# Spreading small constants by TensorE products, key sums in four column tiles, stores in pairs on two queues, and a new order of everything

## The chip, the cores and the metric

The kernel runs on one core of a Trainium2 chip. A core has five engines that run side by side: TensorE (PE) for matrix products, VectorE (DVE), ScalarE (ACT), GpSimd (POOL) and SyncE (SP), which here only issues DMAs. ACT issues DMAs too, in line with its own work. The metric is the device time of one execution in microseconds (us), the median of several runs.

## The reference

Two stages follow each other. The first is a linear attention with a product feature map, for 4 batches of 4 heads, 1088 tokens and 32 channels; the second is a two-layer network over the 4352 tokens, with 128 inputs and outputs and 2048 hidden units.

```
a = S1 @ x ; b = S2 @ x                      # 8 numbers each, per token
phi(x) = outer(a, b)                         # 64 features
kv = sum_s phi(k_s) v_s^T ;  z = sum_s phi(k_s)
attn = phi(q) kv / (phi(q) . z + 1e-6)       # per batch and head
x = attn, heads side by side                 # 4352 x 128
h = x @ w_in
out = (max(h,0) + alpha * min(h,0)) @ w_out
```

## The kernel before

All inputs come in as float32. The network is computed in bfloat16 in this form: with g = relu(h), the output is g @ (w_out scaled by 1 − alpha) plus x @ W, where W = w_in @ (w_out scaled by alpha) is computed once (step Wmm). So each 512 tokens need 16 products with w_in (h), 16 relus (r, on ACT or DVE), 16 products with the scaled w_out, w_a (o), one product with W, a transpose out of PSUM (t, on DVE) and a store (s). There are eleven such pieces: 0a, 0b (256 tokens each), 1 to 6 (512 each), 7, 8 and 9 (256 each). Piece 9 multiplies the other way round, so that tokens come out on partitions and no transpose is needed; its two halves of 128 tokens are copied out by t9.0 and t9.1 and stored by s9.0 (SP) and s9.1 (ACT).

Ahead of each piece stands the attention. For the keys of batch b: kbT (a DVE transpose), kbf (the 16 numbers a and b, on TensorE), kbab (transposed back), kbp0 and kbp1 (the products a·b, on DVE or POOL, in tiles kp), kbv (sums of key features with V), kbz, kbzm, kbcw, kbcc (the sums of the keys, folded into the weights fW for the denominators), kbvc, kbvT, kbW (kv laid out as weights). For the queries: qbf, qbg, qbcb, qbs, qbe, qbrc, qbbd (denominators), qbp (products), qbt (transposes), qbn (numerators) and qbx, which is the input of the network. The first 512 tokens of batch 0 go by a shorter path, f0 and f1, so that the network can start early.

Constants are made at the start: ident on POOL, masks from it on DVE, then rowsT on TensorE, which turns S1 and S2 (loaded as rows0 and rows1), and kW, Sab and fW from it. S1rep comes from a third load, rowsS1, and alpha from a load that lays 2048 numbers over the partitions in runs of four. The steps w_in_bf, w_a, w_b, w_hi and w_lo prepare the weights; winT and winTc turn w_in.

The program is a graph of named steps. ORDER is a list, written by a planner, of every step with its engine (`@p` PE, `@d` DVE, `@a` ACT, `@g` POOL, `@s` SP); each engine works its own steps off in the order of that list and waits in place for what a step needs. SLOTS gives each buffer its place; bank 7 of PSUM collects the outputs of one piece after the other, and three buffers oT hold outputs on their way to DRAM. `fill` steps are idle matmuls, and `warm` is a hundred of them. The costs in the graph were used by the planner alone; the kernel on the chip only knows ORDER and SLOTS.

Of the kernel before, what the change touches and what calls it, by code (L numbers as in the profile page):

```python
# [42 lines left out]
class Graph:  # L43


    CLASSES = {"ps": 8, "kT": 2, "kab": 3, "kp": 4, "qT": 2, "gt": 2, "pr": 3, "pt": 2, "dn": 2, "aq": 2, "dt": 2, "rr": 2,
               "rh": 10, "oT": 3, "xT": 4, "zm": 2, "fs": 2, "wb": 2}
    SHAPES = {"kT": ([128, J * 32], F32), "kab": ([128, 9, 2, 32], F32), "kp": ([128, 20, 64], F32),
# [85 lines left out]
    def load(self, name, dst, src, nbytes, eng="sp", rate=290.0, deps=()):  # L134
        def emit(e):
            (self.nc.sync if eng == "sp" else self.nc.scalar).dma_start(dst(), src())
        return self.op("ld." + name, [(eng, 60, 60)], emit, deps, load=nbytes / rate, queue=eng)
# [5 lines left out]
    def loads(self):  # L143
# [3 lines left out]
            f"S{i + 1}", 0, [D, R], [0, H], [1, D]), 4096, "act", 16.0) for i in range(2)]  # L147
# [14 lines left out]
        def v(b, x):  # L162

            n, lo = (9 - x), 18 * x
            return [self.load(f"v{b}.{2 * x + y}", lambda y=y: T[f"v{b}"][64 * x + 32 * y:64 * x + 32 * y + 32, :, x:, :].rearrange("p h j d -> p h (j d)"),
                              lambda y=y: self.dram("v", b * H * S * D + (lo + n * y) * D, [J * D, 32], [S * D, H], [1, n * D]),
                              128 * n * D * 4, rate=260.0) for y in range(2)]
# [8 lines left out]
        for what in self.LOADS:  # L176
# [3 lines left out]
                lambda: self.dram("q", JM * D, [J * D, 128], [H * S * D, B], [1, 2 * D]), 128 * B * 256, rate=150.0)  # L180
# [12 lines left out]
    def constants(self):  # L193
# [8 lines left out]
        def red(dst, src, off, *dims, axis=AX.X):  # L202
# [5 lines left out]
        self.c_mz = self.op("Mz", [("dve", 140, 220)], lambda e: red("Mz", "ident", 0, [2 * R, H], [64, 2], [1, R], axis=AX.XY), [c_id])  # L208
        self.c_e8 = self.op("E8", [("pool", 300, 340), ("dve", 140, 220)], lambda e: self.copy(
            e, self.tl("E8", 0, [64, 2], [8, 8], [1, 8]), self.tl("M8", 0, [0, 2], [1, R], [0, R])), [self.c_m8])  # L210
        b = self.bank()
# [3 lines left out]
            self.tl("kW", 0, [16, 2], [1, 16]), self.ps(b, 0, [0, 2], [1, 16]), self.tl("par2", 0, [1, 2], [0, 16])), [o, self.c_par], [b])  # L215
        self.c_Sab = [self.op(f"Sab{i}", [self.act(64), self.dve(64)], lambda e, i=i: self.copy(
            e, self.tl("Sab", 64 * i, [8, 8], [1, 8]), self.ps(b, 8 * i, *(([1, 8], [0, 8]), ([0, 8], [1, 8]))[i])), [o], [b]) for i in range(2)]
        self.c_S1 = self.op("S1rep", [("pool", 280, 320), ("dve", 210, 290)], lambda e: self.tt(
            e, self.tl("S1rep", 0, [32, 4], [1, 32]), self.tl("rowsS1", 0, [0, 4], [1, 32]), self.tl("Mz", 0, [1, 4], [0, 32]), ALU.mult),
            [L["rowsS1"], self.c_mz], port=1)  # L220
        self.c_fW = self.op("fW", self.ad(128), lambda e: self.copy(e, self.tl("fW", 0, [16, 8], [1, 16]), self.ps(b, 0, [0, 8], [1, 16])), [o], [b])
        self.c_om = self.op("omaT", [("pool", 100, 140), ("dve", 80, 160)], lambda e: (self.nc.vector if e == "dve" else self.nc.gpsimd).tensor_scalar(
            T["omaT"], T["alphaT"], -1.0, 1.0, ALU.mult, ALU.add), [L["alpha"]], port=1)
# [8 lines left out]
    def weights(self):  # L232
# [5 lines left out]
        for i in range(4):  # L238
            def scaled(e, dst, a, i=i):
# [10 lines left out]
                e, self.sb(bw, 0, [DM, 4], [1, DM]), T[f"w_out_f{i}"], self.tl("alphaT", 4 * i, [1, 4], [0, DM]), ALU.mult), [L["alpha"]] + L["w_out", i], [bw], port=1)  # L250
# [21 lines left out]
        o = self.op("Wmm", [self.pe(109 * NC + 10, 170)], wm, lo + wt, [b], ni=32)  # L272
# [6 lines left out]
    def keys(self, b):  # L279
# [18 lines left out]
        else:  # L298
            o = self.op(f"k{b}f", [self.pe(650)], lambda e: feats(e, range(4)), [turns[0], self.c_kW], [bT, bf], ni=32, mode=2)
        o = self.op(f"k{b}ab", [self.dvt(576)], lambda e: nc.vector.transpose(  # L300
            self.sb(bab, 0, [32, 2], [64, 9], [1, 32]), self.ps(bf, 0, [512, 2], [32, 9], [1, 32])), [o], [bf, bab])

        prods = []
        for x, (lo, n) in enumerate(((0, 5), (5, 4))):
            bp = self.buf("kp")

            def pr(e, lo=lo, n=n, bp=bp):
                self.tt(e, self.sb(bp, 0, [64, 4 * n], [8, 8], [1, 8]), self.sb(bab, 64 * lo, [16, 4 * n], [1, 8], [0, 8]),
                        self.sb(bab, 64 * lo + 8, [16, 4 * n], [0, 8], [1, 8]), ALU.mult)
            prods.append((self.op(f"k{b}p{x}", [self.pool(256 * n), self.dve(256 * n)], pr, [o], [bab, bp], port=1), lo, n, bp))  # L310
# [8 lines left out]
        z = self.op(f"k{b}z", [self.pe(310)], zs, [o], [bab, bz], ni=36, mode=1)  # L319
# [5 lines left out]
        o = self.op(f"k{b}cw", [self.pe(230)], lambda e: self.mm(self.ps(bc, 0, [1, 32]), T["S1rep"], self.sb(bzm)), [zm, self.c_S1], [bzm, bc], ni=4, mode=1)  # L325
# [12 lines left out]
        for x, (p, lo, n, bp) in enumerate(prods):  # L338
# [6 lines left out]
            o = self.op(f"k{b}v{x}", [self.pe(128 * n + 30)], kv, [p, o] + L["v", b], [bp, bk], ni=16 * n, mode=1)  # L345
# [399 lines left out]
```

## Time and profile before

| | |
|---|---|
| median of 3 runs | 120.55 us (120.3 to 121.59) |
| profiled execution | 121.51 us, its span 119.7 us |
| PE busy | 102.6 us, 86% |
| DVE, ACT, POOL busy | 82.1, 65.2, 46.3 us |
| read from HBM, written | 8.81 MB, 2.23 MB |
| mean granted clock of TensorE | 0.901 |

The span runs from the first instruction of the profiled execution to the last; the execution's own time holds about 1.8 us more. In the slices of the page one digit stands for a fortieth of the span, 3 us. In the chain and the timeline a row gives the start in us, the duration in us, the engine, the line of the kernel, and output<-input. Tile numbers such as oT__101 tell buffers apart. A window row gives its length, then for each engine busy us and the number of instructions, then the granted clock, the mean busy share of the DMA engines and GB/s. Most matmuls are recorded under one line, that of the helper `mm`, so they are told apart by tiles.

### The profile page before, as it was taken

The numbers are of one execution on the slowest core, as the hardware profiler recorded it, in microseconds if no ns is written. First come the engines' busy times: TensorE is split into PE (matmuls) and PEld (weight loads), VectorE is DVE, ScalarE is ACT, GpSimd is POOL, SyncE is SP. The second block draws the span as 40 slices with busy tenths as digits, with TensorE's granted clock in tenths as the row PEclk, the third lists the DMA queues.
The fourth block names the chain that finished last, engine by engine and source line by source line (L and its number), as shares of the span: only waits on it lengthen the run. The fifth ranks groups of instructions, "written<-read, shape, count | busy, mean of one in ns | idle before, by whom it ended". The sixth has DMA issues, their size and how long they took to land.

```text
span 119.7 us, 3722 instructions
## 1 busy us (share of the span) xinstructions
PE 102.6 (86%) x1559; PEld 61.9 (52%) x1574; DVE 82.1 (69%) x144; ACT 65.2 (54%) x125; POOL 46.3 (39%) x49
## 2 busy tenths in 40 slices
PE   7339889989999998999999999999999999997000
PEld 7214568457776665445445544544444457887000
DVE  3217805789797799878997849779869966674000
ACT  0410136979954686767548447778336637764000
POOL 2011942959999599226940003980010300000000
PEclk9975555599999999999999999999999999999855
DMA  3988999999950002200400000273320000453310
GB/s 109 275 292 239 265 379 274 259 221 234 244 124 11 0 3 38 60 5 9 78 0 5 0 5 0 44 125 55 53 35 5 0 0 0 70 94 52 58 27 16
DMA packets 24096, 11.28 MB, mean 94 GB/s; under 512 B 19088, under 2 KB 21392, under 8 KB 24080
## 3 DMA queue, kind: packets, MB, share of 16 engines
q1 hardware_dynamic: 23136, 10.95, 37.8%
q8 instruction: 12, 0.20, 0.7%
q10 hardware_dynamic: 944, 0.10, 0.6%
q14 instruction: 4, 0.03, 0.1%
HBM read 8.81 MB, written 2.23 MB: 92 GB/s over the span
## 4 chain that ended last, share of the span: by engine, by line
PE 46%; DMA 14%; POOL 11%; DVE 11%; SPq 7%; issue 3%; ACT 2%; ACTq 1%; DVEq 0%; POOLq 0%
PE ps L130 44%; DMA alphaT<-in_moe_alpha_dram 5%; SPq L561 5%; DMA v<-in_v_dram 5%; DVE pr__77 L127 3%; POOL kp__69 L127 2%; POOL w_hl L127 2%; POOL pr__77 L127 2%; POOL kp__70 L127 2%; POOL dn__82 L127 2%; DVE gt__75 L418 2%; DMA out_dram<-oT__101 1%; DMA out_dram<-oT__100 1%; DMA out_dram<-oT__102 1%; SPq L568 1%
## 5 line engine op out<-in xcount | busy, mean ns | idle before, releaser
L130 PEld LDWEIGHTS <-w_in_bf 128*128 128x128 bf16 x176 | 16.8, 98 | 13.1 <-issue 1.3
L130 PE MATMUL ps<-xT__103,w_in_bf 128*128 128x256 bf16 (+1 forms) x94 | 22.2, 325 | 0.5 <-ACT w_in_bf L122 0.2
L130 PEld LDWEIGHTS <-w_a 128*128 128x128 bf16 x160 | 15.4, 98 | 13.3 <-issue 3.0
L130 PE MATMUL ps<-xT__104,w_in_bf 128*128 128x256 bf16 (+1 forms) x62 | 15.6, 325 | 0.1
L516 ACT ACTIVATE rh__91<-ps 128x512 bf16<-128x512 f32 x14 | 8.4, 599 | 3.6 <-PE ps L130 3.5
L516 ACT ACTIVATE rh__93<-ps 128x512 bf16<-128x512 f32 x13 | 7.8, 599 | 4.6 <-PE ps L130 3.9
L516 ACT ACTIVATE rh__92<-ps 128x512 bf16<-128x512 f32 x13 | 7.8, 598 | 3.0 <-PE ps L130 3.0
L127 POOL TENSOR_TENSOR kp__70<-kab__66 128x1024 f32<-128x1024 f32 x3 | 7.2, 2384 | 5.3 <-DVE kab__66 L300 5.2
L516 ACT ACTIVATE rh__90<-ps 128x512 bf16<-128x512 f32 x11 | 6.6, 600 | 4.7 <-PE ps L130 4.7
L127 POOL TENSOR_TENSOR pr__78<-gt__75 128x512 f32<-128x512 f32 x6 | 7.7, 1299 | 0.9 <-DVE gt__75 L127 0.9
L127 POOL TENSOR_TENSOR pr__77<-gt__75 128x512 f32<-128x512 f32 x5 | 5.8, 1170 | 5.1 <-DVE gt__75 L127 4.9
L130 PE MATMUL ps<-const-bfloat16-1.0 128*32 128x32 bf16 (+1 forms) x107 | 6.4, 214 | 1.6 <-issue 0.9
L127 POOL TENSOR_TENSOR dn__82<-gt__75 128x256 f32<-128x256 f32 (+2 forms) x4 | 2.2, 554 | 13.2 <-DVE gt__75 L418 13.2
L518 DVE TENSOR_SCALAR rh__96<-ps 128x512 bf16<-128x512 f32 x9 | 6.1, 676 | 1.3 <-PE ps L130 1.3
L122 ACT CAST w_in_bf<-w_in_f 128x512 bf16<-128x512 f32 x4 | 4.5, 1113 | 4.6 <-DMA w_in_f<-in_moe_w_in_dram 4.6
L516 ACT ACTIVATE rh__97<-ps 128x512 bf16<-128x512 f32 x10 | 6.0, 600 | 1.7 <-PE ps L130 1.7
L424 POOL TENSOR_SCALAR dn__82<-dn__82 128x32 f32<-128x32 f32 (+2 forms) x5 | 1.4, 274 | 14.2 <-PE ps L130 12.6
L418 DVE STREAM_TRANSPOSE gt__75<-ps 128x1024 f32<-128x1024 f32 (+2 forms) x5 | 4.9, 975 | 2.6 <-PE ps L130 1.8
L516 ACT ACTIVATE rh__94<-ps 128x512 bf16<-128x512 f32 x9 | 5.4, 598 | 2.2 <-PE ps L130 2.1
L130 PE MATMUL ps<-pt__80,kvW 32*32 32x256 f32 (+2 forms) x320 | 6.4, 332 | 0.0
L287 DVE STREAM_TRANSPOSE kT__64<-k 128x1088 f32<-128x1088 f32 (+2 forms) x5 | 5.3, 1069 | 1.3 <-DMA k<-in_k_dram 1.3
L130 PE MATMUL ps<-rh__91,w_a 128*128 128x256 bf16 (+1 forms) x22 | 6.1, 322 | 0.1
(168 smaller groups left out, 235.2 us busy)
## 6 DMA issues: line engine op xcount, KB each, us to landing
q<-in_q_dram SPq DMA_DIRECT2D x3, 512.0 KB, 8.1
k<-in_k_dram SPq DMA_DIRECT2D x4, 288.0 KB, 6.2
v<-in_v_dram SPq DMA_DIRECT2D x8, 144.0 KB, 6.6
k<-in_k_dram SPq DMA_DIRECT2D x4, 256.0 KB, 5.4
v<-in_v_dram SPq DMA_DIRECT2D x8, 128.0 KB, 6.8
w_out_f<-in_moe_w_out_dram SPq DMA_DIRECT2D x4, 256.0 KB, 4.7
w_in_f<-in_moe_w_in_dram SPq DMA_DIRECT2D x4, 256.0 KB, 5.8
out_dram<-oT__102 SPq DMA_DIRECT2D x12, 64.0 KB, 1.9
```

Source lines behind the costliest of these rows:

```text
L122: nc.scalar.copy(dst, src)
L127: (self.nc.vector if e == "dve" else self.nc.gpsimd).tensor_tensor(out=dst, in0=a, in1=b, op=what)
L130: self.nc.tensor.matmul(out, w, x, start=start, stop=stop, skip_group_check=True)
L287: turns.append(self.op(f"k{b}T{x}", [self.dvt(32 * n)], lambda e, lo=lo, n=n: nc.vector.transpose(self.sb(bT)[:, 32 * lo:32 * lo + 32 * n] ...
L418: o = self.op(tag + "g", [self.dvt(4 * n)], lambda e: nc.vector.transpose(self.sb(bG, 0, [n, 4], [1, n]), self.ps(bF, 0, [512, 4], [1, n]) ...
L424: o = self.op(tag + "e", [("pool", 100, 140), ("dve", 90, 170)], lambda e: (nc.vector if e == "dve" else nc.gpsimd).tensor_scalar_add(self ...
L516: nc.scalar.activation(self.sb(br), self.ps(bh, 0, [1, 512]), ACTF.Relu)
L518: nc.vector.tensor_scalar_max(self.sb(br), self.ps(bh, 0, [1, 512]), 0.0)
L561: self.nc.sync.dma_start(self.tokens(b, j, n, i), self.sb(bt, 0, [32, n], [1, 32], p=(32 * i, 32)))
L568: self.nc.sync.dma_start(self.dram("out", (JM + jj) * DM + 32 * i, [J * DM, 32], [S * DM, B], [1, 32]), self.sb(bt, 32 * jj, [64, B], [1, ...
```

## The change

- **Constants by products.** The load rowsS1 and its product on POOL go. S1 is spread over the partitions by a product of a repeated identity (M8T, a POOL copy) with the rows already loaded (S1x on TensorE), then masked by DVE (S1rep). Alpha is loaded as 16 rows of 128 numbers; it is masked into `am` (POOL), and four small products with a mask (aT on TensorE) spread it; alphaT and omaT are copied out of PSUM. rows1 is loaded by SP, rows0 and alpha by ACT.
- **Key sums.** kbab lays a and b out in two blocks of 32, and kbz computes with 32 instead of 64 columns of weights, in four column tiles instead of two.
- **Key products.** kbp is cut by head into four steps (batch 0: two times four), so that they can be dealt out to DVE and POOL. For batches 1 to 3 one kp tile holds all nine groups; there are two such tiles instead of four smaller ones.
- **Stores.** Every store step issues two DMAs; a piece has two such steps (piece 7 four), each on SP's or ACT's queue.
- **Last piece.** Piece 9 is two chains, 9a and 9b, with an output bank each.
- **Order and slots.** The planner's costs are changed (a load is taken as 450 or 620 ns of its queue and 1800 ns of latency), and ORDER and SLOTS are new throughout. On SP the loads now come as k0.0, rows1, k0.1, q0.0, v0.3, v0.1, w_in3, v0.2, v0.0, w_out0, w_in2, w_out1, q0.1, w_in1, w_in0, k1.1, k1.0, v1.3, w_out2, w_out3, and so on; v1.2 is the 31st load on SP, behind parts of batches 2 and 3.

```
-        L["rowsS1"] = self.load("rowsS1", lambda: T["rowsS1"], lambda: self.dram("S1", 0, [0, 16], [D, R], [1, D]), 16384, "act", 16.0)
-        L["alpha"] = self.load("alpha", lambda: T["alphaT"].rearrange("p (a b) -> p a b", b=4),
-                               lambda: self.dram("moe_alpha", 0, [4, 128], [512, 4], [1, 4]), 8192, "act", 8.0)
+        L["alpha"] = self.load("alpha", lambda: T["arow"], lambda: self.dram("moe_alpha", 0, [128, 16], [1, 128]), 30000, "act", [L["rows"][0]])
...
+        s1 = self.op("S1x", [self.pe(260, 110)], lambda e: self.mm(self.ps(b1, 0, [1, 128]), T["M8T"], T["rows"]), [m8t, o], [b1], ni=4, mode=1)
+        self.c_S1 = self.op("S1rep", [self.dve(128)], lambda e: self.nc.vector.tensor_mul(
+            self.tl("S1rep", 0, [32, 4], [1, 32]), self.ps(b1, 0, [32, 4], [1, 32]), self.tl("Mz", 0, [1, 4], [0, 32])),
+            [s1, self.c_mz], [b1])
...
+        am = self.op("am", [self.pool(512), self.dve(512)], lambda e: self.tt(
+            e, self.tl("am", 0, [128, 4], [1, 128]), self.tl("arow", 0, [0, 4], [1, 128]), self.tl("mkp", 0, [1, 4], [0, 128]), ALU.mult),
+            [L["alpha"], mk[0]], port=1)
+        def at(e):
+            for c in range(4):
+                self.mm(self.ps(ba, c, [4, 4]), self.tl("am", c, [4, 128]), T["mkq"])
...
         def zs(e):
             for j in range(9):
                 p = (0, 64) if j == 0 else (0, 128)
-                self.mm(self.ps(bz, 0, [1, 32], p=(64 * (j % 2), 64)), self.sb(bab, 64 * j, [1, 64], p=p),
-                        self.sb(bab, 64 * j + 8, [16, 4], [1, 8], p=p), start=j < 2, stop=j > 6)
+                self.mm(self.ps(bz, 0, [1, 32], p=(32 * (j % 4), 32)), self.sb(bab, 64 * j, [1, 32], p=p),
+                        self.sb(bab, 64 * j + 32, [1, 32], p=p), start=j < 4, stop=j > 4)
...
+            parts, work = store(bt, part == "b")
+            for x in range(0, len(parts), 2):
+                def st(e, two=parts[x:x + 2]):
+                    for to, at in two:
+                        (nc.scalar if e == "act" else nc.sync).dma_start(to(), at())
+                self.op(f"s{name}.{x // 2}", [("sp", 490, 2000), ("act", 520, 2000)], st, [o], [bt], nd=2, load=work, lat=1450)
...
 ORDER, the steps on PE up to the first pieces:
+warm fill rowsT S1x fill k0f0 k0f1 fill aT f0.a f0.b k0z fill k0v0 f1.a k0fz k0cw f1.b winT1 k0v1 f1.den f0.den k0VT
+fill f0.num fill q0f k0vT h0a.2 winT0 h0a.4 h0a.0 h0a.6 f1.num k1f ... Wmm ... W0a q1f o0b.12 W0b ... k2f q0n k1v0 h1.5
 the last stores:
+SP:  s6.0 s5.0 s6.1 s7.3 s7.0 s7.2 s8.0 s9a.1 s9b.0      ACT: s4.1 s7.1 s8.1 s9a.0 s9b.1
```

More of the change, by code (lines that the diff above doesn't have):

```diff
@@ L337, in keys @@
         o = None
-        for x, (p, lo, n, bp) in enumerate(prods):
+        for x in range(0, len(prods), H):
+            lo, n, bp = prods[x][1:]
             def kv(e, lo=lo, n=n, bp=bp):
@@ new lines @@
+winT1@p f1.ac@a k0v1@p f1.m@d ld.w_in0@s w_hi0@a f1.den@p k0Vc@a q0T1@d f0.den@p k0vc@a k0VT@p winTc1@a ld.k1.1@s f1.dT@d w_a1@g w_in_bf1@a k0V@d
+fill@1 f0.num@p f0.dT@d k0cc@d w_a0@g f1.e@d ld.k1.0@s f0.e@d f0.rc@d f1.rc@d ld.v1.3@s f0.rr@d w_b1@g fill@3 q0f@p w_in_bf0@a k0vT@p ld.w_out2@s
+f0.x@d w_lo0@g w_hi1@a h0a.2@p k0W@a winT0@p ld.w_out3@s r0a.2@a h0a.4@p q0g@d ld.v1.0@s k1T0@d r0a.4@a w_lo1@g q0cb@g ld.k2.0@s h0a.0@p h0a.6@p
+ld.q1.0@s f1.num@p w_b2@g ld.v2.2@s f1.rr@d r0a.6@a q0s@d k1f@p ld.k2.1@s f1.x@d o0a.6@p h0a.14@p w_a2@a k1ab@d q0e@g h0a.8@p q0rc@d winTc0@d w_b3@g
```

209 lines of the change are left out of this document (95 added, 114 removed), and 16 rows, old and new, of the table SLOTS.

## The prediction

> **What bounds the kernel now.** I read the slices of the page first, then the chain that ended last, in order of time, then the timeline around the two ends of the dense stretch.
>
> ```profile
> span 119.7 us, 3722 instructions
> ...
> PE   7339889989999998999999999999999999997000
> ...
> PEclk9975555599999999999999999999999999999855
> DMA  3988999999950002200400000273320000453310
> ```
>
> Three stages are to be seen. In the first eight slices (24 us) TensorE works at half its clock while the DMA is full. Then it is full at the whole clock for 29 slices. In the last three it is empty, and only a few transfers run.
>
> ```profile
> 8.06 0.26 PE L212 MATMUL ps<-ident,rows 16*128 16x16 f32 x1 [3.76 <-DMA rows<-in_S_dram]
> ...
> 11.53 1.49 DVE L127 TENSOR_TENSOR kp__69<-kab__66 128x1280 f32<-128x1280 f32 x1
> 11.58 3.25 POOL L127 TENSOR_TENSOR kp__70<-kab__66 128x1024 f32<-128x1024 f32 x1 [5.18 <-DVE kab__66 L300]
> ...
> 15.65 1.45 PE L130 MATMUL ps<-kp__69,v 64*32 64x64 f32 x40 [0.33 <-DMA v<-in_v_dram]
> ...
> 24.41 0.60 PE L130 MATMUL ps<-xT__103,w_in_bf 128*128 128x256 bf16 x4
> ...
> 109.67 0.39 PE L130 MATMUL ps<-w_a,rh__95 128*128 128x128 bf16 x4
> ...
> 115.49 1.72 SPq L576 DMA_DIRECT2D out_dram<-oT__101  x4
> ```
>
> The dense stretch runs from the first hidden-layer product, 24.41, to the end of the last output product, 109.67 + 0.39 = 110.06: 85.65 us. The span is thus 24.41 + 85.65 + 9.64 of tail. The dense stretch holds what TensorE has to do; the two ends hold waits. The chain names them:
>
> ```profile
> 2.03 6.25 DMA alphaT<-in_moe_alpha_dram
> ...
> 9.62 5.90 DMA v<-in_v_dram
> ...
> 15.65 5.71 PE ps L130 x140
> ...
> 108.69 1.43 DMA out_dram<-oT__102
> ...
> 110.11 0.26 ACT oT__100 L122
> ...
> 113.36 1.64 DMA out_dram<-oT__101
> ...
> 115.17 0.29 DVE oT__101 L124
> ```
>
> At the front, a load issued on SP waited for the alpha load of 8 KB to land (6.25 us), so the V load behind it left at 9.62 and landed at 15.51; TensorE took it up at 15.65. At the back, the two last copies wait for stores: the buffer of t9.0 (oT__101) was still being stored by tile 8, whose four DMAs stood on SP behind the eight of tile 7. TensorE was done at 110.06, and that copy ran at 115.17.
>
> **The change, part by part. The start.** The first TensorE step that counts, rowsT at 8.06, waited for the second of the rows loads; ACT issued it last of four, behind the short-run rowsS1 and alpha. Now rowsS1 is gone, rows0 is first on ACT, and rows1 is second on SP behind k0.0. Its landing is unknown. One bound is the landing of the load that it stands behind, the other the alpha load's 6.25:
>
> ```profile
> k<-in_k_dram SPq DMA_DIRECT2D x1, 288.0 KB, 2.8
> ```
>
> Issued at about 1.2, it lands between 4.0 (after 2.8) and 7.4 (after 6.25). I take 4.5, near k0.0, since no short-run load is left ahead of it: 3.6 us earlier than 8.06, bounds 4.1 and 0.7.
>
> The added S1x, M8T and the masks are small steps of the rowsT kind (0.26 us) on engines that idle here; I cost them at nothing, and at 1 us together if that cover is gone. One is placed dangerously: aT, which spreads alpha, stands on TensorE ahead of f0.a. If alpha lands as late as today (issued at 1.4, landing at 7.6, then the product am of about 1 us on POOL), f0.a and all TensorE work behind it wait until about 9; with 16 runs instead of 2048 I take it as landed before 6, so free.
>
> The V wait: today rowsT to the end of the DVE product of the keys is 13.02 − 8.06 = 4.96 us, so V came 2.6 us after it was needed. In the new order 1600 KB (k0, half of q0, v0, one quarter of w_in) must come before v0 is whole.
>
> ```profile
> 0.00:5.00 5.00, 3.21 (x101) 2.88 (x102) 1.71 (x7) 1.49 (x2) 0.69 (x6) 1.00 0.61 174
> 5.00:10.00 5.00, 1.94 (x18) 0.68 (x18) 1.40 (x3) 0.42 (x2) 0.64 (x2) 0.73 0.82 255
> ...
> 30.00:35.00 5.00, 5.00 (x95) 3.58 (x80) 4.26 (x7) 4.42 (x9) 4.92 (x6) 1.00 0.95 211
> ```
>
> At 174 and then 255 GB/s that is 0.87 MB by 5 us and the other 0.77 MB by 8.0; with some spread of the ends of V's four parts I take 9.3. The products, cut in four by head, end at 4.5 + 5.2 = 9.7 (0.2 for the cutting). So k0v0 starts at 9.7 instead of 15.65.
>
> From there to the first hidden-layer product it is 24.41 − 15.65 = 8.76 us today, a chain of small fp32 products, copies and casts. The new order adds winT1 ahead of it and the wait of winT1 for two quarters of w_in, seventh and eleventh on SP:
>
> ```profile
> 23.59 0.98 PE L263 MATMUL ps<-identb,w_in_bf 128*128 128x128 bf16 x8
> ...
> 17.05 1.11 ACT L122 CAST w_in_bf<-w_in_f 128x512 bf16<-128x512 f32 x1 [4.62 <-DMA w_in_f<-in_moe_w_in_dram]
> ```
>
> winT1 costs 0.98. Another count, by ACT: w_in2 lands at about 11.5, its cast ends near 13, then stand in order two copies, the copy k0Vc (which waits for k0v1 on TensorE until about 15), k0vc, winTc1 (as long as a cast, I take it) and two casts (2.2): 19. Both ways h0a starts at about 9.7 + 8.76 + 0.98 = **19.4**, 5.0 us earlier. Bounds: 17 with all small loads early and the whole clock, 24 with rows and alpha late.
>
> **The dense stretch.** 85.65 us today. winT1 (0.6 at full clock) and q0f (0.5) have moved ahead of h0a: −1.1. The key sums, k1z to k3z, change from two column tiles to four:
>
> ```profile
> 31.24 0.89 PE L130 MATMUL ps<-kab__66 64*64 64x32 f32 x18
> 32.06 0.61 PE L130 MATMUL ps<-xT__104,w_in_bf 128*128 128x256 bf16 x4
> ...
> 37.88 1.00 PE L130 MATMUL ps<-kp__69,v 64*32 64x64 f32 x40
> 38.93 0.65 PE L130 MATMUL ps<-kp__70,v 128*32 128x64 f32 x32
> 39.52 0.28 PE L130 MATMUL ps<-xT__103,W_bf 128*128 128x256 bf16 x1
> 39.64 1.24 PE L130 MATMUL ps<-xT__105,w_in_bf 128*128 128x512 bf16 x4
> 40.72 0.38 PE L130 MATMUL ps<-rh__90,w_a 128*128 128x256 bf16 x2
> 40.94 0.38 PE L130 MATMUL ps<-rh__96,w_a 128*128 128x256 bf16 x2
> ```
>
> Today 18 records take 32.06 − 31.24 = 0.82, 45 ns each. Products in four column tiles, with twice the moving columns, take (39.52 − 37.88) / 72 = 23 ns each. So 0.4 less each, 1.2 for three; bounds nothing and 1.5. The Trainium skill speaks against it: "TensorEngine Tiling (Array Packing)", Performance Considerations, says that a matmul has a floor of some 60 cycles and warns against taking a tiling factor from a dimension that is already small; with 32 moving columns it would give no gain, and the sum would be 1.2 longer. The trace disagrees as far as 23 against 45 ns go.
>
> The slices show TensorE at nine tenths nearly throughout this stretch, so little more can be won; what can be lost is the cover for an earlier start. The work that feeds TensorE before h1 is the same, and POOL has a queue without gaps in the new order after w_hi1 (19.4 + 0.6): w_lo1 to w_lo3, w_b2, w_b3, q0p00, q0p01 and all four of k1p, which k1v0 waits for, ahead of h1.
>
> ```profile
> 28.81 1.04 POOL wb__112 L127
> 29.85 1.12 POOL w_hl L127
> ...
> 31.41 2.09 POOL pr__77 L127 x2
> ...
> 34.62 2.35 POOL kp__69 L127
> 36.97 1.91 POOL kp__70 L127
> ```
>
> 3 × 1.12 + 2 × 1.04 + 2.09 + 4.26 = 11.8, with three short ones about 12.9: k1v0 at about 32.9, and with its 1.6 h1 at 34.5. TensorE by itself: h1 came at 39.64, 15.2 after h0a; the new order puts the eight o0b (40.94 − 40.72 = 0.22 each) and W0b (half of one) ahead of it, 1.9, and takes out 1.1 and 0.4, so 15.6: 35.0. The two are level, and any wait on one shows. I add 1.0 of new stalls; bounds 0 and 5. Dense stretch: 85.65 − 1.1 − 1.2 + 1.0 = 84.35, ending at **103.75**.
>
> Stores on ACT's queue: seven pairs of about 0.9 (four DMAs took 1.72 on SP), three of them before the tail, stand in front of relus. DVE's relus and the ten rh buffers cover them; without that cover three pairs would cost 2.7.
>
> **The tail.** After the last product: copy t9b (0.29), two DMAs on each of two queues instead of four (1.72 / 2 = 0.86), and what follows the last issue today, 119.7 − 117.21 = 2.49. With 0.1 between: 3.8 instead of 9.64. That needs free queues and buffers. t9b takes the buffer of tile 7. Between t7's and the end TensorE has about 5.5 us of work; SP then issues three pairs of tile 7 (2.6), s8.0 and s9a.1 (0.9 each), and is free at about the time t9b is done. The price of a queue that is late is 0.9 a pair. Bounds 3.5 and 6.
>
> ```profile
> 110.39 1.55 DMA out_dram<-oT__100
> ```
>
> A store lands about 1.55 after its issue, so tile 7's buffer is clear about 0.5 before the end of TensorE's work.
>
> **The sum.** Span 19.4 + 84.35 + 3.8 = 107.55 against 119.7. The profiled execution took 121.51, 1.81 more than its span, so 109.4 by that footing. It lies 0.96 above the median of the three runs, 120.55; I give the time on the median's footing: **108.5**. The runs spread from 120.3 to 121.59, so about 1% is what a measurement tells from no change.
>
> **The rivals.**
>
> A. The clock stays whole from the start.
>
> ```profile
> 7.00:8.00 1.00, 0.00 (x0) 0.00 (x0) 0.00 (x0) 0.00 (x0) 0.00 (x0) 0.66 0.88 312
> ...
> 24.00:25.00 1.00, 1.00 (x20) 0.77 (x24) 0.69 (x3) 0.36 (x1) 0.93 (x2) 0.81 1.10 212
> ```
>
> The clock fell at about 7.3 (0.66 over that microsecond), while TensorE waited 3.76 us for rows, and rose at 24.4. With rowsT at 4.5 that idle time is gone. TensorE's part of the front (about half of the 8.76) shrinks, but ACT's queue stands: the copy k0Vc comes 0.9 earlier and h0a at 18.2, so 107.3. Against it: the small products did not raise the clock from 8 to 24 although TensorE shows as busy. The Trainium skill, "TensorE: Matmul & The Clock Gate", Part 1, gives the gate a free-running window of about 3.4 us, whole after a busy one and half after an idle one. By that rule the trace agrees (24.4 − 7.3 is five windows), and the new front, without an idle window, would keep the clock.
>
> B. The engines that feed TensorE become the bound until h1. For it: POOL at 4.92 of 5 us in the row of 30 to 35 above, and ACT at 4.42. Each wait there is passed on, h1 comes 3 to 5 us later than I put it, and the time is 111 to 114.
>
> C. The small loads don't come earlier, so that the spreading by products doesn't do what it is for: rowsT at 7 or aT holding TensorE until 9. Then h0a stands at 22 to 24, and only the tail is won: 111.5 to 113.5. Against it: 16 runs of 512 bytes.
>
> D. Slower. k1v0 is queued on TensorE ahead of h1, and its last V part, v1.2, is put behind 6976 KB (7.14 MB) of others, parts of k2, q2 and k3 among them. It decides only if it lands later than the 32.9 of POOL's queue. At the slowest loading row, 211 GB/s, it comes at 33.8 plus some landing, and costs 1 to 3. To end above 121.75 it would have to land at 46, a rate of 160. With that the time is 122.
>
> **How the numbers follow.** The forecast (106 to 111.5) has 0.62; A 0.12 at 107.3; B 0.15 at 112.5; C 0.08 at 112.5; D 0.03 at 122. The range runs from 104.5 (h0a at 17, no new stalls, a tail of 3.5: 17 + 82.3 + 3.5, with 0.85, is 103.7, not quite reached) to 113.5, which takes in most of B and C. Faster by over 1% is all but D and the far end of B and C: 0.94; the same 0.03; slower 0.03.
>
> **What would show it.** In the profile after: rowsT at 4 to 5; k0v0 near 9.7 and no longer released by V; the first matmul on w_in_bf at 18 to 21; k1z at about 0.4 instead of 0.8; h1 near 35, and POOL without gaps before it; the last matmul at 102 to 106, and under 4.5 us behind it. I am wrong if TensorE shows gaps of over 2 us in all between 20 and 40, if h0a comes after 22, or if the last copy waits for a store again.

## The result, and the profile after

The changed kernel takes **112.34 us** (median of four, 111.99 to 114.84) against 120.42 (four, 119.97 to 121.59): a ratio of 0.929, interval 0.920 to 0.937. Forecast were 108.5 and a range of 104.5 to 113.5. The time lies inside the range, but outside the 106 to 111.5 that had most of the chance. A ratio leaves out executions over 1.5% above the fastest of their kernel, here the profiled one of 114.84, whose end stands 2.5 us later than the median's; the four that this ratio rests on took 111.39 to 112.67.

The page's first part, the rows of the slices:

```profile
span 113.1 us, 3776 instructions
...
PE   7999999999997975999999999999999999999910
...
PEclk9999999999999999999999999999999999999997
DMA  3999999991008870100110350140040240026131
```

TensorE's weak slices at the end are two instead of four, and the loads of the start are done after nine slices. The clock row shows no half clock any more; it will turn out that it can't be believed.

TensorE's timeline of the start, of the first hidden products and of two key sums inside the dense stretch (start, duration, engine, line, output<-input, records):

```profile
4.05 0.28 PE L212 MATMUL ps<-ident,rows 16*128 16x16 f32 x1
4.18 0.77 PE L130 MATMUL ps<-rows,M8T 16*128 16x128 f32 x2
4.88 1.03 PE L130 MATMUL ps<-const-bfloat16-1.0 128*128 128x512 bf16 x2
5.85 1.21 PE L130 MATMUL ps<-kT__64,kW 64*32 64x288 f32 x16
6.99 1.46 PE L130 MATMUL ps<-const-bfloat16-1.0 128*128 128x512 bf16 x3
8.38 2.03 PE L130 MATMUL ps<-mkq,am 16*128 16x4 f32 x8
10.34 1.16 PE L130 MATMUL ps<-qT__71,Sab 32*64 32x128 f32 x32
...
12.58 1.45 PE L130 MATMUL ps<-kp__69,v 64*32 64x64 f32 x40
...
21.93 0.39 PE L130 MATMUL ps<-xT__101,w_in_bf 128*128 128x256 bf16 x2
...
25.71 0.51 PE L130 MATMUL ps<-kab__66 64*32 64x32 f32 x18
26.15 0.39 PE L130 MATMUL ps<-xT__102,w_in_bf 128*128 128x256 bf16 x2
...
38.17 2.20 PE L130 MATMUL ps<-xT__101,w_in_bf 128*128 128x512 bf16 x9
...
43.60 0.33 PE L130 MATMUL ps<-kab__66 128*32 128x32 f32 x14 [1.79 <-issue]
```

rowsT comes at 4.05. No DMA releases k0v0 any more, but it starts at 12.58, not 9.7, and TensorE has no gap before it: it works fills (1.03, 1.46, 0.61) and aT (2.03) first. The first hidden product is at 21.93. k1z takes 26.15 − 25.71 = 0.44 instead of 0.82. Inside k2z TensorE stands for 1.79 for nothing that the profile shows.

The end of the chain that ended last (start, duration, what):

```profile
105.91 1.60 DMA out_dram<-oT__98
107.52 0.32 SPq L560
...
107.94 1.58 DMA out_dram<-oT__98
109.52 0.29 DVE oT__100 L124
```

The last copy still waits for a store, and ahead of it SP waits for the landing of a DMA that ACT had issued at 105.91. (The row just ahead of the copy is a store of oT__98. In the compiled program the copy waits for the stores of tile 7, oT__100, and the last of these is the one that SP issued at 107.52.) The last product ended at 107.72, so the tail is 113.1 − 107.72 = 5.38 instead of 9.64.

By the three terms of the sum: start 21.93 (forecast 19.4), dense stretch 85.79 (84.35), tail 5.38 (3.8), together 5.55 more than the forecast's span of 107.55. Before they were 24.41, 85.65 and 9.64, so between the two profiles 2.5 us are won at the start and 4.3 in the tail, and nothing in the dense stretch, where 1.79 is the stop inside k2z. How much of that is owed to the S1 products, the pairs of stores, the two chains of piece 9 and the order is not shown, since no run takes these back one by one.

### The profile page after: what moved, and what is told of

Same layout as the page of the kernel before. It is cut to its first block, busy times and chain, and to the rows that moved or that the text cites. A ratio compares the mean times of both kernels' runs of the same rounds, so it can differ in the third digit from the quotient of the medians.

```text
span 113.1 us, 3776 instructions
## 1 busy us (share of the span) xinstructions
PE 104.2 (92%) x1585; PEld 61.6 (54%) x1585; DVE 81.6 (72%) x148; ACT 66.2 (59%) x130; POOL 46.5 (41%) x57
## 4 chain that ended last, share of the span: by engine, by line
PE 75%; POOL 8%; issue 4%; ACT 4%; DMA 3%; DVE 2%; SPq 0%
PE ps L130 74%; DMA out_dram<-oT__98 3%; POOL w_hl L127 2%; POOL kp__69 L127 2%; POOL pr__75 L127 2%; ACT w_in_bf L122 1%; DVE pt__78 L465 1%; DVE gt__73 L436 1%; POOL wb__110 L127 1%; PE ps L279 1%; ACT winT L122 1%; PE ps L376 1%; ACT w_hl L122 0%; POOL dn__80 L127 0%; ACT rh__94 L532 0%
## 5 line engine op out<-in xcount | busy, mean ns | idle before, releaser
L130 PE MATMUL ps<-xT__101,w_in_bf 128*128 128x512 bf16 (+1 forms) x112 | 25.9, 333 | 0.0
L130 PE MATMUL ps<-xT__102,w_in_bf 128*128 128x256 bf16 (+1 forms) x64 | 15.7, 326 | 0.0
L127 POOL TENSOR_TENSOR kp__69<-kab__66 128x576 f32<-128x576 f32 x10 | 11.6, 1183 | 3.4 <-DVE kab__66 L316 3.4
L127 POOL TENSOR_TENSOR pr__75<-gt__73 128x512 f32<-128x512 f32 x8 | 8.9, 1129 | 2.0 <-DVE gt__73 L127 1.8
L532 ACT ACTIVATE rh__88<-ps 128x512 bf16<-128x512 f32 x11 | 6.6, 599 | 4.7 <-PE ps L130 4.2
L532 ACT ACTIVATE rh__95<-ps 128x512 bf16<-128x512 f32 x13 | 7.9, 607 | 1.2 <-PE ps L130 1.2
L130 PE MATMUL ps<-const-bfloat16-1.0 128*32 128x32 bf16 (+1 forms) x111 | 7.7, 222 | 0.8 <-PEq L732 0.8
L532 ACT ACTIVATE rh__91<-ps 128x512 bf16<-128x512 f32 x11 | 6.6, 602 | 2.8 <-PE ps L130 2.8
L532 ACT ACTIVATE rh__90<-ps 128x512 bf16<-128x512 f32 x11 | 6.5, 594 | 1.4 <-PE ps L130 1.0
L532 ACT ACTIVATE rh__96<-ps 128x512 bf16<-128x512 f32 x10 | 6.0, 597 | 2.0 <-PE ps L130 2.0
L442 POOL TENSOR_SCALAR dn__80<-dn__80 128x32 f32<-128x32 f32 (+1 forms) x4 | 1.6, 389 | 13.5 <-DVE dn__80 L440 13.4
L130 PE MATMUL ps<-rh__90,w_a 128*128 128x256 bf16 (+1 forms) x24 | 6.9, 327 | 0.0
L130 PE MATMUL ps<-rh__88,w_a 128*128 128x256 bf16 (+1 forms) x23 | 6.5, 325 | 0.0
L127 POOL TENSOR_TENSOR dn__80<-gt__73 128x128 f32<-128x128 f32 (+2 forms) x3 | 1.5, 500 | 12.0 <-DVE gt__73 L436 12.0
L465 DVE STREAM_TRANSPOSE pt__78<-pr__75 128x1024 f32<-128x1024 f32 (+1 forms) x5 | 5.6, 1117 | 1.0 <-POOL pr__75 L127 1.0
L127 POOL TENSOR_TENSOR pr__76<-gt__73 128x512 f32<-128x512 f32 x6 | 6.3, 1065 | 0.0
```

The source lines that it names most:

```text
L127: (self.nc.vector if e == "dve" else self.nc.gpsimd).tensor_tensor(out=dst, in0=a, in1=b, op=what)
L130: self.nc.tensor.matmul(out, w, x, start=start, stop=stop, skip_group_check=True)
L442: o = self.op(tag + "e", [("pool", 100, 140), ("dve", 90, 170)], lambda e: (nc.vector if e == "dve" else nc.gpsimd).tensor_scalar_add(self ...
L465: ts.append(self.op(f"{tag}t{x}", [self.dvt(64 * g)], lambda e, bP=bP, x=x: nc.vector.transpose(self.sb(bPT, 64 * g * x, [1, 64 * g]), sel ...
L532: nc.scalar.activation(self.sb(br), self.ps(bh, 0, [1, 512]), ACTF.Relu)
```

## The experiments

The table has each kernel's median, its ratio to the kernel before on the same chip, and from its profile where the greater part of k0v0 starts (the first two of 40 products may come earlier), the first hidden product h0a, the first one of 512 tokens h1, the end of the last product, and the tail behind it, in us.

| kernel | median | ratio, interval | k0v0 | h0a | h1 | last product | tail |
|---|---|---|---|---|---|---|---|
| before | 120.42 | | 15.65 | 24.41 | 39.64 | 110.06 | 9.64 |
| after | 112.34 | 0.929 (0.920 to 0.937) | 12.58 | 21.93 | 38.17 | 107.72 | 5.38 |
| e1 same | 113.07 | 0.943 (0.934 to 0.952) | 12.67 | 22.09 | 38.24 | 106.87 | 5.53 |
| e2 no fills | 112.23 | 0.935 (0.928 to 0.942) | 11.07 | 20.46 | 37.08 | 104.61 | 5.59 |
| e3 alpha in short runs | 112.54 | 0.937 (0.931 to 0.942) | 11.62 | 20.97 | 37.20 | 105.22 | 6.18 |
| e4 own buffer | 112.37 | none | 12.49 | 22.38 | 38.08 | 105.62 | 6.08 |
| e5 one queue | 114.95 | 0.959 (0.952 to 0.966) | 12.58 | 22.02 | 38.16 | 105.70 | 6.50 |
| e6 two column tiles | 114.48 | none | 13.37 | 22.73 | 38.98 | 107.25 | 5.85 |
| e7 products on DVE | 113.03 | 0.941 (0.933 to 0.950) | 10.94 | 21.09 | 38.00 | 105.56 | 6.24 |
| e8 one pair to SP | 112.97 | 0.941 (0.933 to 0.948) | 10.98 | 20.12 | 36.28 | 104.50 | 5.20 |
| e9 tail | 113.75 | 0.951 (0.942 to 0.959) | 12.59 | 21.95 | 38.20 | 105.74 | 5.86 |
| e10 no fills, tail | 113.99 | 0.948 (0.939 to 0.957) | 11.55 | 21.29 | 37.48 | 106.48 | 6.02 |
| e11 also alpha | 112.67 | 0.938 (0.930 to 0.946) | 10.79 | 20.13 | 36.99 | 104.86 | 5.84 |
| e12 other queues | 112.43 | 0.935 (0.928 to 0.942) | 12.23 | 21.62 | 38.04 | 105.59 | 5.21 |

e1 to e4, e5 to e8, and e9 to e11 shared a chip each; the kernel before took 120.47, 119.86, 120.22 and, with e12, 120.47. The same kernel came out at 0.929 and 0.943, so a ratio alone parts two versions only where they lie over 1.5% apart. The profiles part them better, with two limits. One is the tail: the changed kernel, e1, e2, e3, e6 and e7 issue their last stores in the same order, and their tails run from 5.38 to 6.24, so a tail between these is no effect of an edit. The other is the dense stretch from h0a to the last product, which runs from 83.24 to 85.79 over all versions. For e4 and e6 there is no ratio: one of four executions of each, of 109.35 and 111.75, lies 2.3% or more under the other three.

**e1, the changed kernel again.**

> The changed kernel as it is, once more, for a second profile to set the edits against. In the first one TensorE waited 1.79 us in the middle of k2z (41.8 to 43.6) with nothing that the profile shows as the cause, and the last store pair left SP at 109.87. Theory 1: that wait belongs to that execution, and without it the span is 110 to 111. Theory 2: it belongs to the order, and stands here again at the same step. Both: time near 112.2, first hidden-layer product near 22, k0v0 near 12.6.

Its front repeats to 0.2 us, but by another path. In the changed kernel's profile the key products were done at 10.97 and TensorE came to k0v0 1.6 later; in e1 TensorE was there first and waited for DVE. DVE's rows of e1, and PE's:

```profile
8.19 0.71 DVE L387 STREAM_TRANSPOSE qT__71<-q 128x512 f32<-128x512 f32 x1 [2.10 <-DMA q<-in_q_dram]
8.82 0.74 DVE L316 STREAM_TRANSPOSE kab__66<-ps 128x576 f32<-128x576 f32 x1
9.60 2.99 DVE L127 TENSOR_TENSOR kp__69<-kab__66 128x320 f32<-128x320 f32 x4
```
```profile
12.67 1.45 PE L130 MATMUL ps<-kp__69,v 64*32 64x64 f32 x40 [0.47 <-DVE kp__69 L127]
```

In ORDER the transpose q0T0 of the first half of q stands ahead of k0ab on DVE, and here its load let it start only at 8.19, against 6.25 in the other execution. So two bounds of the front lie close together, and that the two k0v0 agree is chance. The stop inside k2z is 0.89 instead of 1.79; in e5 the same 18 products run in 0.51 without a stop.

**e2, the fills.**

```
-amkq@d fill@1 / kW@d fill@2 / k0p00@d fill@3 / alphaT@a fill@1 / fill@1 f0.num@p / w_b1@g fill@3      (six places, 11 products)
+amkq@d        / kW@d        / k0p00@d        / alphaT@a        / f0.num@p        / w_b1@g
```

> Leaves out the eleven idle matmuls (fill) behind the warm-up. Theory 1 (TensorE itself bounds the front, at half rate: three idle matmuls took 1.46 us at 6.99 while aT, whose operand was ready at 4.83, stood behind them): k0v0 comes 1.2 to 1.6 us earlier than in the changed kernel, the first hidden-layer product 1 to 2 us earlier, time 110.2 to 111.2. Theory 2 (the idle matmuls bring the clock up; it rose near 19.3): without them the matmuls stay at half rate for longer, the first hidden-layer product comes no earlier, time 112 to 114.

k0v0 comes 1.5 earlier and now waits for DVE (PE's timeline of e2):

```profile
11.07 1.44 PE L130 MATMUL ps<-kp__69,v 64*32 64x64 f32 x38 [0.53 <-DVE kp__69 L127]
```

So of the 2.9 us that k0v0 was late, the fills held 1.5, and with them gone the key products are the next bound (q0T0 had waited 1.14 for q and started at 6.62). At h1 the gain is 1.1; the time's gain lies inside the intervals. Theory 2 is not refuted by this: the first two hidden products took 0.61 here and 0.39 in the changed kernel, as if the rate had come up later without the fills; but in e10, also without fills, they took 0.38.

**e3, alpha as before.**

```
-load alpha as 16 rows of 128 into arow; amkp, amkq, am, aT, alphaT
+load alpha in runs of four into alphaT, as in the kernel before
```

> Takes back the part of the change that spreads alpha by products: alpha is loaded in runs of four numbers as before the change, second on ACT's queue, and am, aT and the copy of alphaT are left out; all else as changed. Theory 1 (aT's 2.03 us on TensorE, in front of f0.a, cost the front about 1.6 us): k0v0 1.5 to 2 us earlier, the first hidden-layer product 1 to 2 us earlier, time 110 to 111.2. Theory 2 (the short-run load holds a queue slot for six us and delays the loads of V and weights behind it, as in the kernel before): k0v0 is released by V again, time 113 to 115.

Without aT k0v0 comes 1.0 earlier than in e1 and again waits for DVE; V doesn't hold it. The time is that of e1 or 0.5 less. So in the new order the short-run load no longer holds V, and spreading alpha by products brings nothing that these runs show: TensorE pays 2.03 us for it.

**e4, a buffer of its own for the last output tile.**

```
-"oT": 3,   ... 6, 2]
+"oT": 4,   ... 6, 3]
```

> A fourth output buffer, used by 9b alone, so that its copy needs no store of piece 7 to have landed. Theory 1 (the tail is held by that buffer: the copy waited until 109.52, TensorE was done at 107.7): the copy follows TensorE at once, and the time falls by 1 to 1.6. Theory 2 (SP's queue is the bound: its pair for 9b left only when SP was free, at 109.87): the copy is early, but the last pair leaves SP no earlier, and the time falls by 0.2 at most.

The last copy ran at 105.72, right behind the last product, and the tail was no shorter (6.08): the last pair left SP only at 108.78. In this execution the buffer was not the bound of the tail; SP's queue was. The execution of 109.35 is the shortest of any version, and the profile is of one of 113.51; what made the other short is not known.

**e5, one queue.**

```
-s0a.1@a s1.0@a s4.1@a s7.1@a s8.1@a s9a.0@a s9b.1@a
+s0a.1@s s1.0@s s4.1@s s7.1@s s8.1@s s9a.0@s s9b.1@s
```

> All stores go back to SP's queue; the pairs, the loads, the spreading products and the key sums stay as changed. Theory (two queues are worth something, but less than I put it): with one queue the six stores that ACT had in the tail, about 0.9 us each, stand on SP too, while the waits of SP's DMAs for DMAs of ACT's queue go away; the tail behind the last product grows from 5.4 us to about 7 to 8 and the time by 2, to 114 to 115. Rival (the semaphores that the two queues share take back all that the second queue gives): SP issues a pair in 0.9 us instead of up to 1.6, the tail stays at 5.5 or falls, and the time is that of the changed kernel, 112.3 to 113.

SP's timeline:

```profile
104.53 1.86 SPq L560 DMA_DIRECT2D out_dram<-oT__98  x4
106.48 1.78 SPq L560 DMA_DIRECT2D out_dram<-oT__99  x4
108.36 1.76 SPq L560 DMA_DIRECT2D out_dram<-oT__100  x4
```

Twelve DMAs without a wait, 0.45 each, and the last one leaves at 110.12, 4.42 behind the last product. The tail is 6.5, the longest of all, but only 0.3 above the longest with the changed kernel's order; the theory's 7 to 8 was too much. Against e7 and e8 of the same chip the time is 1.9 to 2.0 longer, as the theory had it. The profile doesn't show where most of that lies: it is of the shortest of four executions, 114.02 of 114.02 to 115.5.

**e6, two column tiles.**

```
-kbz: weights [1, 32], output p = (32 * (j % 4), 32);  Mz over [32, 4]
+kbz: weights [1, 64], output p = (64 * (j % 2), 64);  Mz over [64, 2]
```

> The key sums go back to weights of 64 columns in two column tiles, as in the kernel before; all else stays as changed. My sum put the three later key sums at 0.4 us each, so the dense stretch should be longer by 1.2 and k1z should take 0.8 again instead of 0.44; the time 113.5 to 114. Rival (the gain is swallowed by waits that follow, since TensorE has to wait for its feeders between 35 and 45 us anyway): k1z takes 0.8 but the last product ends no later, and the time is 112.3 to 113.

```profile
26.39 0.89 PE L130 MATMUL ps<-kab__66 64*64 64x32 f32 x18
27.21 0.39 PE L130 MATMUL ps<-xT__102,w_in_bf 128*128 128x256 bf16 x2
```

k1z takes 0.82 again. So the 0.4 for a key sum is shown. And k0z, which I had left out of the sum, takes 1.42 instead of 0.68 (from 11.48, ahead of k0v0, which starts 0.79 later than in e5). What this is worth in the time is not shown: from h0a to the last product it is 84.52, in the middle of 83.24 to 85.79, and the profile is of an execution of 114.89, while another took 111.75, level with the changed kernel. Theory and rival stay undecided.

**e7, key products of batch 0 on DVE alone**, without fills.

```
-k0p10@g k0p12@g k0p13@g
+k0p10@d k0p12@d k0p13@d
```

> No filling products, as in the second experiment, and in addition the three key products of batch 0 that POOL took are put on DVE, behind its own. Theory (DVE and POOL take turns on one path to the memory, so a product on one doubles the time of that on the other): eight products of 0.4 to 0.5 us each on DVE alone are done in about 3.5 us, each of DVE's about 0.5 instead of 0.75; the second half of k0v0 starts 0.5 to 1 us earlier than in the second experiment (11.07), and the first hidden product at 19.5 to 20 instead of 20.46. Rival (the two engines are independent, and DVE's products are long by themselves): DVE's products stay at 0.75, the last of eight ends 2 us later than now, and the first hidden product comes at 21.5 to 22.5.

DVE's rows:

```profile
7.27 0.71 DVE L387 STREAM_TRANSPOSE qT__71<-q 128x512 f32<-128x512 f32 x1 [1.35 <-DMA q<-in_q_dram]
...
8.68 1.70 DVE L127 TENSOR_TENSOR kp__69<-kab__66 128x320 f32<-128x320 f32 x4
10.30 0.42 DVE L127 TENSOR_TENSOR kp__70<-kab__66 128x256 f32<-128x256 f32 x1
```

The four products take 1.70 alone and 2.99 with three of POOL's beside them. The theory of one shared path is right in its size. The gain at k0v0 is lost, since the first half of q landed 0.65 later in this execution and q0T0 stands ahead of k0ab on DVE; and DVE, with three products more, lengthened the way from k0v0 to h0a from 9.39 to 10.15. As a change it brings nothing.

**e8, one pair of stores to SP.**

```
-s8.1@a
+s8.1@s
```

> One pair of stores, the second of tile 8, moves from ACT's queue to SP's; all else stays as changed. In the compiled program a DMA waits for the one eight before it in program order, whichever queue that stands on; with this move SP's DMAs of the tail hardly wait for DMAs of ACT any more. Theory (those waits across the queues are what made SP's six DMAs of tile 7 take 4.7 us instead of 2.6): SP issues them in 0.45 each, and although it has two DMAs more, the last pair leaves it about 1 us earlier than in the changed kernel; the tail is 4.2 to 4.7 instead of 5.4 to 5.6 and the time 111.3 to 112. Rival (SP is bound by the time of its own issues, and the waits are beside it): two more DMAs on SP are 0.9 more, the tail is 6.3 and the time 113 to 114.

SP's six DMAs of tile 7 take 3.35 instead of 4.69, the last copy runs 0.28 behind the last product (at 104.78, still behind the landing of a store), and the tail is 5.2 although SP has two DMAs more: between theory and rival, though only 0.2 below the shortest with the changed kernel's order. The front of this execution is the surprise, with nothing changed there. PE's timeline, then the clock row of the page:

```profile
4.78 0.61 PE L130 MATMUL ps<-const-bfloat16-1.0 128*128 128x512 bf16 x2
5.32 0.86 PE L130 MATMUL ps<-kT__64,kW 64*32 64x288 f32 x16
6.11 0.83 PE L130 MATMUL ps<-const-bfloat16-1.0 128*128 128x512 bf16 x3
6.86 2.02 PE L130 MATMUL ps<-mkq,am 16*128 16x4 f32 x8
8.82 0.69 PE L130 MATMUL ps<-qT__71,Sab 32*64 32x128 f32 x32
...
10.98 1.17 PE L130 MATMUL ps<-kp__69,v 64*32 64x64 f32 x38 [0.48 <-DVE kp__69 L127]
```
```profile
PEclk9999556999999999999999999999999999999995
```

The same instructions take 0.61 for 1.03, 0.83 for 1.46, 0.69 for 1.16: here TensorE had its whole rate until about 10, in the profile of the changed kernel only half of it from 4.9 on. h0a is 1.8 earlier. Only aT takes the same, 2.02 and 2.03. The rate alone doesn't bring that gain: in e4 the fills took 0.61 and 0.82 too, but q0T0 started at 8.03 instead of 6.52, k0v0 waited for DVE until 12.49, and h0a came at 22.38.

**e9, the tail.**

```
-"oT": 3 ...   s7.2@s  s8.1@a
+"oT": 4 ...   s7.2@a  s8.1@s
```

> The tail alone: the third pair of stores of tile 7 goes to ACT's queue, the second pair of tile 8 to SP's, and the last output tile has a fourth buffer of its own. SP's DMAs of the tail then hardly wait for ACT's, SP has 12 DMAs in the tail as in the changed kernel, and the last copy waits for no store. Theory (the tail was longer than my 3.8 by SP's waits for DMAs of the other queue, 1.3, and by nothing else of size): SP issues its DMAs at 0.46 each and the last pair leaves it within 1.7 us of the last product; the tail is 4.1 to 4.4 against 5.4 to 5.6, the time 111.0 to 111.6. Rival (ACT's queue is now the late one, or its relus wait behind the extra pair): the last product comes up to 1 us later, or the last pair on ACT does, and the time stays at 112.3 to 113.

Neither: the tail is 5.86, no shorter than with the changed kernel's order (5.38 to 6.24). I had overlooked one wait of SP for ACT in the compiled program. ACT's timeline with a pair as a group and its second DMA by itself, then SP's with the four DMAs of tile 8 as a group and the second of them by itself:

```profile
103.87 0.81 ACTq L560 DMA_DIRECT2D out_dram<-oT__100  x2
...
104.23 0.45 ACTq L560 DMA_DIRECT2D out_dram<-oT__100  x1
```
```profile
104.81 2.83 SPq L560 DMA_DIRECT2D out_dram<-oT__98  x4
...
106.33 0.32 SPq L560 DMA_DIRECT2D out_dram<-oT__98  x1
```

In the program SP's second DMA of tile 8 waits for the second DMA of ACT's pair of 103.87. That left ACT at 104.23, and SP goes on at 106.33, 2.10 later. With e5's steady 0.45 that DMA would have left 1.1 earlier. The last pair left SP at 109.53, 3.8 behind the last product.

**e10 and e11, front and tail together.**

```
e10: e2 and e9
e11: e2, e3 and e9
```

> The filling products removed (as in the second experiment) together with the new tail. If front and tail are separate terms of the sum, the gains add: from 112.2 without fills, 1.2 to 1.4 less in the tail, 110.8 to 111.0. Rival (the gain of the fills is within the spread of the executions): the time is that of the new tail alone, 111.0 to 111.6.

> As the one before, and in addition alpha is loaded in short runs again, so that TensorE doesn't spread it (eight products, 2.0 us, ahead of the first query product); am, aT and the copy of alpha are left out. Theory (without the fills the first value product waits for DVE's key products, which POOL's share the path with, and TensorE's 2.0 us stand in time in which it would wait): the first value product of batch 0 starts where it does with them, 11.0 to 11.1 for its greater part, and the time is within 0.5 of the experiment before. Rival (TensorE's queue is the bound of the front by itself): the first value product starts at 9.6 to 10, the first hidden product at 19 to 19.5, and the time is 109.5 to 110. Third case (the short-run load holds up the loads again): the time is 111.5 or more.

Since e9's tail is no gain, e10's sum fails with it: 113.99. Its front is later than e2's by 0.4 to 0.8: the transpose of the second half of k waited 1.35 for its load and came at 6.02 instead of 4.60. e11 is 1.3 below e10, more than theory allowed (0.5) and less than the rival's, with intervals that overlap; k0v0 starts at 10.79 and waits 0.47 for DVE. TensorE's queue alone is thus not the bound of the front once the fills are gone.

**e12, queues laid out by the waits**: as e11, but s8.1 back on ACT.

> As the experiment before (no filling products, alpha by short runs, a fourth output buffer), but the tail's queues are laid out by the waits that the compiled program has: only the third pair of tile 7 goes from SP to ACT, the second pair of tile 8 stays on ACT, so ten DMAs on each queue. Worked out DMA by DMA (0.46 us for an issue on SP, 0.41 on ACT, and a DMA that has to wait for the one eight before it starts 2.2 us after that one's issue, sizes read from the changed kernel and the new tail of the ninth experiment), the tail is 5.3 for the changed kernel, 5.1 with the eighth experiment's queues, 5.7 with those of the ninth, and 4.2 here. Theory (the waits between the queues are the whole of the tail's miss): 4.0 to 4.5 from the last product to the end, against 5.84 in the experiment before, and a time 1.3 to 1.6 below its 112.67: 111.1 to 111.4. Rival (something else holds the last DMAs, the time from an issue to its landing above all): the tail is 5.2 or more and the time 112.0 to 112.8.

The tail is 5.21: the rival's number. (The front was 1.4 later than in e11, since q landed at 7.78; the time is 0.2 less.) ACT's rows:

```profile
103.72 0.81 ACTq L561 DMA_DIRECT2D out_dram<-oT__100  x2
104.62 0.89 ACTq L561 DMA_DIRECT2D out_dram<-oT__98  x2
106.27 0.81 ACTq L561 DMA_DIRECT2D out_dram<-oT__99  x2
107.47 0.79 ACTq L561 DMA_DIRECT2D out_dram<-oT__101  x2
```

t9a was copied at 104.67 + 0.29 = 104.96, and its pair left ACT at 106.27. My count had missed that the first DMA of a pair waits for its predecessor by eight too, here the second DMA of the pair of 103.72 (the wait stands in an instruction of its own). The pair of 104.62 ended at 105.51, so t9a's stood 0.76 for that wait, and the last pair of ACT left behind it, at 107.47. Without it the tail would be 4.45 by my estimate, 5.21 − 0.76. The reckoning had come out at 5.3, 5.1 and 5.7 for the changed kernel, e8 and e9, whose tails had been measured before it (5.38 and 5.53, 5.20, 5.86); for e12, the only one that it forecast, it was 1.0 too short. No kernel without these waits was run. That they alone keep the tail from 3.8 is therefore argued, not shown.

No version with a ratio beat the changed kernel by more than the intervals; e2, e3, e11 and e12 are level with it.

## Why the prediction was right, and where it was 4 us short

**The loads: right.** rowsT at 4.05 (forecast 4.5), V no longer the bound, alpha's product am done at 4.83. Of rival C only the number came (111.5 to 113.5, and h0a at 21.93 to 22.09 where it had 22 to 24), not its cause.

**The start of k0v0: the step that failed**, 12.58 for 9.7. The key products' late end, 10.97 for 9.7, is 1.3 of it, and TensorE's own queue the other 1.6. Two terms were mis-sized, and a third was left out.

- "The products, cut in four by head, end at 4.5 + 5.2." They ended at 10.97, 6.9 behind rowsT. Most of the excess stands in these rows of the changed kernel's timeline, of DVE and of POOL:

```profile
7.17 0.78 DVE L316 STREAM_TRANSPOSE kab__66<-ps 128x576 f32<-128x576 f32 x1 [0.20 <-PE ps L130]
7.98 2.99 DVE L127 TENSOR_TENSOR kp__69<-kab__66 128x320 f32<-128x320 f32 x4
```
```profile
8.03 2.60 POOL L127 TENSOR_TENSOR kp__70<-kab__66 128x256 f32<-128x256 f32 x3 [3.20 <-DVE kab__66 L316]
```

  Before, DVE made its half in one piece of 1.49 and POOL's of 1024 took 3.25, which is DVE's 1.49 and 1.76 of its own. POOL came second, and only DVE's half was awaited. Cut up, the two take turns: DVE's four at 0.425 (e7) and POOL's three at 0.44 (1.76 / 4) are 3.02, and DVE's four are spread over 2.99. I put 0.2 on the cutting; it cost 1.5. The rows of before, a product of 3.25 beside one of 1.49, held the hint. The Trainium skill, "SBUF — State Buffer", section "SBUF: two separate sides", says of a DVE instruction with two SBUF inputs and a GpSimd instruction that reads SBUF, as both are here, that whichever starts first gets the shared ports for its whole length and the other blocks; the trace agrees, 1.70 against 2.99.
- "small steps ... I cost them at nothing." The wait for alpha did not come, but aT itself is eight records of 0.25, 2.03 us, at whole and at half rate alike, and the fills on TensorE ahead of k0v0 are 1.03 + 1.46 + 0.61. I had not priced the fills at all, in an order that moves them in front of the work. e2 and e3 put both at 1.0 to 1.6 of k0v0's start; the effects overlap, since behind either stands DVE.
- q0T0 was not in the sum at all. It stands ahead of k0ab on DVE, and with q's landing its start ran from 5.90 (e11) to 8.19 (e1). In e1, e2, e3, e4, e8, e11 and e12 k0v0 waited for DVE and started 3.04 to 3.07 behind the start of the key products. No run moved q0T0 behind them, so what that would bring is open.

**From k0v0 to h0a: right**, 9.35 for 8.76 + 0.98 = 9.74.

**The clock (rival A).** It came in part and not always: whole rate to about 10 in e8 and e4, not in the changed kernel's profile. h0a came 1.8 us earlier in e8 and 0.45 later in e4, where q was late. The record doesn't tell what decides the rate. For the stretch from 14 to 19 the windows of the changed kernel and of e8 say

```profile
14.00:19.00 5.00, 5.00 (x112) 3.81 (x108) 2.74 (x5) 1.72 (x5) 3.37 (x4) 1.00 1.05 317
```
```profile
14.00:19.00 5.00, 5.00 (x108) 2.93 (x101) 3.50 (x11) 3.60 (x7) 2.77 (x3) 0.57 1.06 309
```

a clock of 1.00 and of 0.57, while the same products (16 of qT and Sab in 0.73, the eight of winT1 in 1.03) take the same time in both. The rate is read from the durations. The Trainium skill, "TensorE: Matmul & The Clock Gate", Part 1, warns that these records are unreliable; the trace agrees. Its rule that the rate is halved after an idle window, with which the prediction set rival A, held in e8 to about 10 and not in the changed kernel's profile, where TensorE shows as busy for 8.53 of the 8.53 us from 4.05 to 12.58.

**The dense stretch: right in size.** 83.2 to 85.8 over all kernels, forecast 84.35. h1 came 16.24 behind h0a (forecast 15.6 and 1.0 of stalls). Rival B is right in that the chain runs over ACT and POOL from 18.4 to 33.4, but TensorE lost little by it: 7.91 of 8 us busy from 22 to 30, 7.34 from 30 to 38. Its numbers came too (h1 3.2 later than 35.0, a time in 111 to 114), but 2.5 of the 3.2 are the late start. Of rival D nothing shows: k1v0 starts at 36.90 without a wait for V. Of the changed kernel's 85.79, 1.79 is the stop inside k2z, which comes and goes with the execution (1.79, 0.89, none in e5); its cause stays open.

**Key sums: right**, 0.44 for 0.82, with k0z forgotten (e6). That they shorten the time is not shown.

**The tail: right in kind, 1.6 short.** "SP then issues three pairs of tile 7 (2.6)." It took 4.69 for them:

```profile
103.15 0.43 SPq L560 DMA_DIRECT2D out_dram<-oT__100  x1
...
105.24 0.79 SPq L560 DMA_DIRECT2D out_dram<-oT__100  x2
...
106.45 0.32 SPq L560 DMA_DIRECT2D out_dram<-oT__100  x1
106.82 0.44 SPq L560 DMA_DIRECT2D out_dram<-oT__100  x1
107.52 0.32 SPq L560 DMA_DIRECT2D out_dram<-oT__100  x1
```

Between them are 1.66, 0.43 and 0.26 of standing. In the compiled program the DMAs of both queues take eight completion semaphores in turn, and a DMA waits for the one eight before it in program order. SP's at 105.24 and 107.52 wait for DMAs that ACT had issued at 102.66 and 105.91; the 0.43 is put down to no DMA. I had asked whether queues and buffers were free, not what a DMA waits for besides its data. The rest was right: 2.21 from the last issue to the end (2.49), 2.1 to 3.0 over all versions.

**The range and the signs.** The lower end was added up wrongly: without new stalls the dense stretch is 83.35 by the prediction's own terms (83.05 with the largest gain in the key sums), not 82.3, and the sum 104.4 to 104.7, not 103.7. Of the three signs of being wrong, one came: the last copy waited for a store. h0a missed its limit of 22 by 0.07, and passed it in e1 (22.09). TensorE's gaps between 20 and 40 were 0.8 in all, under the limit of 2.

So the forecast held to within its range because the loads, the dense stretch and the key sums did, and it was 3.8 short of the median by the front and the tail. In the profile none of the three terms made up for another: start, dense stretch and tail all came out longer than forecast. DVE's shared products and SP's waits stand in the profiles of all versions that keep that deal and these queues; the rate of the front and q's landing differ from one execution to the next.

## What to carry to other kernels

When work is cut in pieces for DVE and POOL, add up both engines' pieces: whoever waits for one of them waits for nearly all. Look at what stands ahead of the critical work on its engine, too: a transpose whose load landed 1.9 us later in one of two executions of the same kernel held up the key products behind it. Price idle matmuls and small spreading products like any other instruction when an order moves them ahead of the first useful work. When stores are dealt to two queues, write down for each DMA which earlier one its semaphore waits for, the pair's first one too, and add its landing (1.6 to 2.6 us from its issue in the waits above).

## What the hardware showed that I had not expected

- Eight small products with 128 columns of weights and four moving columns took 0.25 us each, at whole and half rate alike (2.02 in e8, 2.03 in the changed kernel).
- The granted clock's record can say 1.00 while the matmuls run at half rate (14 to 19 us, above).
- TensorE stopped for 1.79 and 0.89 us inside a key sum without anything in the profile to wait for, in two executions of the same kernel.
